# Eight rotating W2 buffers, and an output projection split into four full row tiles and a 64-row remainder

## The chip, the cores and the metric

The kernel runs on one core of one Trainium2 chip. The metric is the device time of one execution in microseconds (us): before the change 562.51 us, the median of three runs (562.33 to 562.85). A core has five engines that run their own instruction streams and meet through semaphores: TensorE (PE, with its weight loads listed apart as PEld), VectorE (DVE), ScalarE (ACT), GpSimd (POOL) and SyncE (SP), which here only issues DMAs. ACT issues DMAs as well.

## The reference

One transformer block in parallel form, with bf16 inputs: sequence S = 2048, width D = 576, H = 32 heads of Dh = 18, sliding window W = 256, feed-forward width F = 4608.

```python
xn = layernorm(x)
q, k, v = split(xn @ wqkv)                        # 32 heads of 18
p = softmax(mask(q @ k.T * 18**-0.5))             # causal, window of 256
attn = (p @ v) @ wo                               # output projection, 576 x 576
glu  = (silu(xn @ w1) * (xn @ w3)) @ w2           # 576 -> 4608 -> 576
out  = x + attn + glu
```

## The kernel before, in words

The sequence is cut into four chunks of 512 rows (c = 0 to 3). Each chunk goes through three stages on PE, and PE runs them strictly one after the other:

- **Projections** (`proj_part`, L437): q, k, v of the chunk from the normalised, transposed input `xnT`. The depth of 576 is handled as nine pieces of 64 rows; two matmuls of 64 rows each stand at array rows 0 and 64 (`tile_position`), write two different PSUM banks and run side by side. I call two such matmuls a pair.
- **Units** (`unit_pairs`, L664): 36 units per chunk, one for each 128 columns of W1 and W3; nine pairs of 512 columns each. Between the pairs the code lays single attention steps: `scores` (L557), `exps` on ACT (L566), `masks` on POOL (L593), and, when the exponentials of two head groups are there, a `pv` block (L614). `unit_tanh` (L673, ACT) and `unit_h` (L679, L682, DVE) turn the two PSUM banks of a unit into one 128-row slice of `hT`. Three PSUM jobs of two banks rotate over the units.
- **P2** (`p2_list` and `p2_item`, L687 to L731): the second feed-forward matmul and the output projection, summed in the same four PSUM banks `ACC[tt]` (tt = 0 to 3 are the blocks of 128 sequence rows). It makes two passes (`half` 0 and 1) over 288 output columns each. A pass runs through nine W2 tiles of 512 rows; a tile is 16 matmuls of 128 rows x 288 columns (L715). In the last tile of a pass each block tt is followed by five matmuls of the output projection (kd = 0 to 4, L721), and then by `out`: DVE adds the residual (L728) and SP stores it (L730).

**W2 tiles** (`load_w2`, L343): four buffers `w2[0..3]` of 288 KB. The first four loads of the program are issued on SP in units 20 to 26 of chunk 0; each later one on ACT, directly after the last matmul of the tile whose buffer it takes, so a load has three tiles of matmuls in which to land.

**W1/W3 tiles** (`load_part`, L312): 36 tiles, nine per chunk, each in six DMAs of 192 KB on SP, in rotating buffers `w13[0..2]`; the fourth tile of chunk 0 alone lands in a part of `hT` that is free then. The counter `owed` spreads the parts: each time a matmul group is put out (`owe_part`), one owed part is issued behind it. The last tile of every chunk lies in `w13[1]`; that buffer is filled again only in the projections of the next chunk, with the third tile of that chunk (first used in unit 8).

**The output projection's input** `oT` has five tiles of 128 partitions. `o_pack` (L639) moves four heads' 18-row blocks of the group pair j (0 to 3) at a time from `od` (two buffers) by DMA: seven blocks fill rows 0 to 125 of tiles 0 to 3, and the last four heads' rows lie in rows 0 to 71 of tile 4. The rest of `oT` and of the weights `wo` is zeroed by four memsets in units 8 to 11 of chunk 0 (L962), and `wo` is loaded in unit 13 by five DMAs.

The order on each engine is the order in which `add` is called in this Python program; there is no scheduler behind it. Waits are worked out from the readers and writers of each named buffer. DMAs that one engine issues are one queue; SP's queue therefore holds W1/W3 parts, the repacking of keys and queries (`span_issue`, L502), the packs of `oT`, x loads and stores in the order of the calls.

The change touches `load_w2`, `o_pack`, `p2_list`, `p2_item`, the calls in the main loop (L829 to L839, L849, L912 to L974) and the numbering of the P2 items (L982).

Of the kernel before, what the change touches and what calls it, by code (L numbers as in the profile page):

```python
# [5 lines left out]
dt = mybir.dt  # L6
# [158 lines left out]
def bass_parallel_sum__sliding_block__glu_gated_swiglu__prompt_kernel(  # L165
# [20 lines left out]
    G = H // 4  # L186
# [11 lines left out]
    with ExitStack() as es:  # L198
# [129 lines left out]
        def load_w13(behind=(), parts=6):  # L328
            for _ in range(parts):
                load_part((), behind)  # L330
# [7 lines left out]
                owed -= 1  # L338
                load_part((op,))

        n2fill = 0

        def load_w2(eng="sp"):  # L343
            nonlocal n2fill
            if n2fill >= NC * 2 * NFC:
                return
            s = n2fill % NW2
            half, fc = divmod(n2fill % (2 * NFC), NFC)
            n2fill += 1
            add(eng, lambda e: e.dma_start(  # L350
                w2[s][:], B_w2[fc * 512:(fc + 1) * 512, half * HD:(half + 1) * HD].rearrange("(fl p) d -> p fl d", p=128)),
                w=[("w2", s)], dma=f"w2_{s}")


        def ln_stats(t, s, part):
# [283 lines left out]
        def o_pack(j, eng):  # L639
            i = j % NOD  # L640
            first = True
            for q in range(4):
                m = 4 * j + q
                if m < 14:
                    t, r0 = 2 * (m // 7), Dh * (m % 7)
                    moves = [(oT[r0:r0 + Dh, t:t + 2, :], od[i][32 * q:32 * q + Dh, :, :])]
                else:
                    r0 = 2 * Dh * (m - 14)
                    moves = [(oT[r0 + Dh * p:r0 + Dh * (p + 1), 4, :], od[i][32 * q:32 * q + Dh, p, :]) for p in range(2)]
                for dst, src in moves:  # L650
                    add(eng, lambda e, dst=dst, src=src: e.dma_start(dst, src),
                        r=[("od", i), "oTz"], dma=f"oT{j}", **{"w" if first else "j": [("oT", j)]})
                    first = False

        def unit_pairs(c, u, n0, n1, b0):

# [30 lines left out]
        def p2_list(c):  # L687

            seq = []
            for half in range(2):  # L690
                base = c * 2 * NFC + half * NFC
# [12 lines left out]

        of_ctr = 0
# [1 line left out]
        def p2_item(c, item, xs):  # L707
            nonlocal of_ctr
            what, half, fc, k, tt, sl, last = item
            d0 = half * HD  # L710
            bank = PS[:, ACC[tt], 0:HD]
            key = [("ps", ACC[tt])]
            if what == "w2":
                f = fc * 4 + k
                add("pe", lambda e: e.matmul(  # L715
                    bank, hT[:, f, tt * 128:(tt + 1) * 128], w2[sl][:, k, :], start=(f == 0), stop=False),
                    r=[("h", f), ("w2", sl)], **{"w" if f == 0 else "j": key})
                if last:
                    load_w2("act")
            elif what == "wo":  # L720
                add("pe", lambda e: e.matmul(  # L721
                    bank, oT[:, k, tt * 128:(tt + 1) * 128], wo[:, k, d0:d0 + HD], start=False, stop=(k == 4)),
                    r=[("oT", j) for j in range(G // 2)] + ["oTz", "wo", "woz"], j=key)
            else:
                o = of_ctr % NOF
                of_ctr += 1
                t = c * TB + tt
                add("dve", lambda e: e.tensor_tensor(ofin[:, o, :], bank, xp[xs[tt]][:, d0:d0 + HD], ALU.add),  # L728
                    r=key + [("xp", xs[tt])], w=[("of", o)])
                add("sp", lambda e: e.dma_start(out2[t * 128:(t + 1) * 128, d0:d0 + HD], ofin[:, o, :]),  # L730
                    r=[("of", o)], dma=f"out{o}")  # L731
# [105 lines left out]
        main, rest = span_main, span_last  # L837
# [5 lines left out]
        for c in range(NC):  # L843
# [23 lines left out]
            def later(u, what):  # L867
                side.setdefault(u, []).append(what)
# [43 lines left out]
            for u in range(NF):  # L912
                at_u = u
                if c == 0 and u == 0:
                    owed += 12
                if u in loads:
                    for i in loads[u]:
                        xslot[(c + 1) * TB + i] = load_x((c + 1) * TB + i)
# [12 lines left out]
                if next_pv in pv_ready and clock >= pv_ready[next_pv] and next_pv < 3:  # L931
                    j = next_pv
                    next_pv += 1
                    banks = job()
                    pv(c, j, banks)
                    clock += PV_COST
                    for g in (2 * j, 2 * j + 1):
                        for s in range(NS):
                            if pt_of[(c, g, s)][0] != "h":
                                free.append(pt_of[(c, g, s)])  # L940
                    later(u, lambda b=banks: (pv_out(b[0], 0), pv_out(b[1], 1), o_scale(0)))
                    later(u + 1, lambda j=j: (o_turn(2 * j, 0), o_turn(2 * j, 1), o_scale(1)))
                    later(u + 2, lambda j=j: o_turn(2 * j + 1, 0))
                    later(u + 3, lambda j=j: (o_turn(2 * j + 1, 1), o_pack(j, "sp")))
                unit_h(u, b0[0])
                for what in side.pop(u, []):
                    what()
# [8 lines left out]
                    ln_apply(t, xslot[t])  # L956
                for span, a, b, n0, n1, eng in late_spans.get(u, []) if c == 0 else []:
                    span(a, b, only=slice(n0, n1), **({"q_eng": eng} if span is main else {"eng": eng}))
                if c == 0 and u in (8, 9, 10, 11):
                    buf, key = ((wo, "woz"), (oT, "oTz"))[(u - 8) // 2]  # L960
                    part = buf[64:128, 4, :] if u % 2 else buf[96:128, 0:4, :]
                    add("dve", lambda e, part=part: e.memset(part.bitcast(dt.float32), 0.0), **{"j" if u % 2 else "w": [key]})  # L962
                if c == 0 and u == 13:
                    for t in range(4):
                        rows = A_wo[252 * (t // 2):252 * (t // 2) + 252, :].rearrange("(s p d) f -> p s d f", p=2, d=Dh)[t % 2, :, :, :]
                        add("sp", lambda e, t=t, rows=rows: e.dma_start(wo[0:126, t, :], rows),
                            r=["woz"], dma="wo", **{"j" if t else "w": ["wo"]})
                    add("sp", lambda e: e.dma_start(wo[0:72, 4, :], A_wo[504:576, :]), r=["woz"], j=["wo"], dma="wo")
# [69 lines left out]
```

## Time and profile before

| what | value |
|---|---|
| time of three runs | 562.51 us median, 562.33 to 562.85 |
| time of the profiled execution | 562.53 us |
| its span in the profile | 560.8 us |
| time outside the span | 562.53 - 560.8 = 1.73 us |
| busy share PE / DVE / ACT / POOL | 99% / 56% / 45% / 29% |
| chunk 0: projections and start, units, P2 | 0 to 22.14, to 102.12, to 143.57 us |
| DMA traffic | 85.83 MB, mean 153 GB/s |

All times of the profile count from the start of the span. A row of a timeline reads: start, length, engine, line, operation, output<-inputs, partitions and columns, count. A row of the chain of waits reads: start, length, what. The length of a matmul group holds the tail of its last matmul (a 288-column matmul is listed with 286 ns, though the next one starts 122 ns later), so rates are read from starts.

### The profile page before, as it was taken

To read this page: it belongs to the slowest core of one execution; us is meant where nothing else is said; L and a number is where in the kernel's file an instruction comes from. 1 tells how busy PE (TensorE), PEld (TensorE's weight loads), DVE (VectorE), ACT (ScalarE), POOL (GpSimd) and SP (SyncE) were. 2 spreads that over 40 slices of the span, in tenths; PEclk is the share of its full clock that TensorE was granted. 3 is DMA by queue.
4 is the path that set the end of the run, shared out by engine and by line. 5 is a ranking of instruction groups with operands and counts; after the bars stand their busy time and mean duration, and the time that the engine had idled before them with its cause. 6 is when DMAs were issued, how large, how long until landed. Compare 5 with 4: busy or idle time off the path is not lost.

```text
span 560.8 us, 15711 instructions
## 1 busy us (share of the span) xinstructions
PE 555.4 (99%) x6767; PEld 343.9 (61%) x6767; DVE 314.8 (56%) x587; ACT 253.1 (45%) x349; POOL 163.1 (29%) x383
## 2 busy tenths in 40 slices
PE   8999999999999999999999999999999999999998
PEld 4445455677665455477766645547777654555776
DVE  7468788710465778851046668883114567767211
ACT  4357776100287776600037776650004676675000
POOL 6313454400034445330003344532000333433000
PEclk9999999999999999999999999999999999999999
DMA  9988879886366467587626754868752675460552
GB/s 249 206 192 179 198 171 203 196 215 176 87 143 145 117 146 165 139 200 206 170 67 139 169 129 111 161 177 189 194 145 59 138 172 131 113 162 12 139 148 64
DMA packets 126685, 85.83 MB, mean 153 GB/s; under 512 B 34024, under 2 KB 124320, under 8 KB 126616
## 3 DMA queue, kind: packets, MB, share of 16 engines
q1 hardware_dynamic: 89076, 63.16, 49.5%
q10 hardware_dynamic: 37540, 21.66, 14.7%
q8 instruction: 53, 0.87, 0.7%
q14 instruction: 16, 0.13, 0.1%
HBM read 71.29 MB, written 2.36 MB: 131 GB/s over the span
## 4 chain that ended last, share of the span: by engine, by line
PE 97%; DMA 2%; DVE 1%; issue 0%; POOL 0%
PE ps L664 50%; PE ps L715 24%; PE ps L437 9%; PE ps L557 6%; PE ps L614 4%; PE ps L721 3%; DMA w<-in_B_w_dram 1%; DMA xp<-in_A_x_dram 0%; DVE xn L370 0%; DVE stats L358 0%; DVE stats L360 0%; DVE mv L361 0%; POOL rstd L364 0%; PE ps L382 0%; DVE ofin L728 0%
## 5 line engine op out<-in xcount | busy, mean ns | idle before, releaser
L664 PE MATMUL ps<-xnT,w 64*128 64x512 bf16 x1400 | 181.3, 376 | 0.1
L664 PE MATMUL ps<-xnS,w 64*128 64x512 bf16 x1120 | 153.9, 376 | 0.0
L715 PE MATMUL ps<-w,hT 128*128 128x288 bf16 x1152 | 147.3, 286 | 0.2 <-DMA w<-in_B_w_dram 0.2
L566 ACT ACTIVATE pt<-ps 128x1024 bf16<-128x1024 f32 (+1 forms) x112 | 113.1, 1010 | 63.4 <-PE ps L557 63.1
L679 DVE SCALAR_TENSOR_TENSOR gs<-th,ps 128x512 bf16<-128x512 bf16 x144 | 97.8, 679 | 77.8 <-ACT th L673 76.7
L715 PEld LDWEIGHTS ps<-w,hT 128*128 128x128 bf16 x1152 | 111.9, 98 | 30.9 <-issue 1.7
L664 PEld LDWEIGHTS ps<-xnT,w 64*128 64x128 bf16 x1400 | 69.9, 94 | 58.6 <-issue 0.5
L593 POOL TENSOR_TENSOR pt<-pt,mk 128x128 int32<-128x128 int32 (+1 forms) x199 | 80.3, 425 | 79.5 <-ACT pt L566 79.5
L682 DVE SCALAR_TENSOR_TENSOR hT<-gs,ps 128x512 bf16<-128x512 bf16 x144 | 98.9, 687 | 5.0
L673 ACT ACTIVATE th<-ps 128x512 bf16<-128x512 f32 x144 | 85.4, 593 | 24.0 <-PE ps L664 23.7
L664 PEld LDWEIGHTS ps<-xnS,w 64*128 64x128 bf16 x1120 | 57.0, 94 | 52.5
L728 DVE TENSOR_TENSOR ofin<-ps,xp 128x288 bf16<-128x288 f32 x32 | 14.6, 457 | 120.2 <-PE ps L721 120.2
L450 ACT ACTIVATE stage<-ps 128x512 bf16<-128x512 f32 x16 | 9.6, 597 | 146.1 <-PE ps L437 143.8
L593 POOL TENSOR_TENSOR hT<-hT,mk 128x128 int32<-128x128 int32 (+1 forms) x31 | 12.4, 421 | 170.7 <-ACT hT L566 170.7
L557 PE MATMUL ps<-qv,kv 64*128 64x320 bf16 (+4 forms) x528 | 52.5, 260 | 0.0
L557 PEld LDWEIGHTS ps<-qv,kv 64*128 64x128 bf16 x528 | 27.3, 94 | 25.8 <-issue 0.3
L437 PE MATMUL ps<-xnT,wp 64*128 64x512 bf16 (+1 forms) x360 | 38.7, 355 | 0.0
L566 ACT ACTIVATE stage<-ps 128x1024 bf16<-128x1024 f32 x24 | 24.6, 1023 | 12.6 <-PE ps L557 12.6
L636 DVE STREAM_TRANSPOSE od<-oq 128x256 bf16<-128x256 bf16 x64 | 25.8, 427 | 6.3 <-POOL oq L629 6.3
L437 PEld LDWEIGHTS ps<-xnT,wp 64*128 64x128 bf16 x360 | 19.0, 94 | 14.1 <-issue 0.7
L721 PE MATMUL ps<-wo,oT 128*128 128x288 bf16 x160 | 24.8, 286 | 0.0
L593 POOL TENSOR_TENSOR stage<-stage,mk 128x128 int32<-128x128 int32 (+1 forms) x42 | 17.0, 423 | 17.4 <-ACT stage L566 17.2
(59 smaller groups left out, 341.9 us busy)
## 6 DMA issues: line engine op xcount, KB each, us to landing
w<-in_B_w_dram SPq DMA_DIRECT2D x210, 192.0 KB, 4.1
w<-in_B_w_dram ACTq DMA_DIRECT2D x68, 288.0 KB, 3.1
xp<-in_A_x_dram SPq DMA_DIRECT2D x29, 144.0 KB, 4.3
out_dram<-ofin SPq DMA_DIRECT2D x32, 72.0 KB, 1.7
xnS<-xnT SPq DMA_DIRECT2D x8, 256.0 KB, 4.3
oT<-od SPq DMA_DIRECT2D x56, 36.0 KB
pt<-in_A_wqkv_dram SPq DMA_DIRECT2D x4, 288.0 KB, 6.5
hT<-in_B_w_dram SPq DMA_DIRECT2D x6, 192.0 KB, 5.1
```

What stands on the lines that cost most here:

```text
L437: op = add("pe", lambda e, out_=out_, st=st, mv=mv, n=n, r0=r0, first=first: e.matmul(out_, st, mv, start=first, stop=(part == 1 and n == ...
L557: add("pe", lambda e, r0=r0, out_=out_, kb=kb, q0=q0, nb=nb: e.matmul(out_, kb4[r0:r0 + 64, g, kb + NV - NB, :] if kb < 0 else kv[r0:r0 + ...
L566: add("act", lambda e: e.activation(pt_slot(sl)[:, 0:w, :], PS[:, SC[0]:SC[1] + 1, 0:w].rearrange("p r q -> p q r"), ACT.Exp, scale=scale) ...
L593: add("pool", lambda e, vb=vb, mm=mm: e.tensor_tensor(vb, vb, mm, ALU.mult), r=(key if n == 0 else []) + ["mk"], **{"w" if n == 0 else "j" ...
L614: add("pe", lambda e, p=p, q=q, pr=pr, sl=sl, g=g, pos=pos, q0=q0, nb=nb, col=col, first=first, n=n: e.matmul(PS[32 * q:32 * q + VW, banks ...
L636: add("dve", lambda e: e.transpose(od[i][:, g % 2, c0:c0 + CH // 2], oq[:, c0:c0 + CH // 2]), r=["oq", "oq0"], **{"j" if half or g % 2 els ...
L664: op = add("pe", lambda e, n=n, r0=r0, r=r, k=k, src=src: e.matmul(PS[:, b0 + r, :], wt[r0:r0 + 64, k, fl * 128:(fl + 1) * 128], src, star ...
L673: add("act", lambda e: e.activation(th[i][:], PS[:, bg, :], ACT.Tanh, scale=0.5), r=[("ps", bg)], w=[("th", i)])
L679: add("dve", lambda e: e.scalar_tensor_tensor(out=gs[i][:], in0=th[i][:], scalar=1.0, in1=PS[:, bg, :], op0=ALU.add, op1=ALU.mult), r=[("t ...
L682: add("dve", lambda e: e.scalar_tensor_tensor(out=hT[:, u, :], in0=gs[i][:], scalar=0.5, in1=PS[:, bu, :], op0=ALU.mult, op1=ALU.mult), r= ...
L715: add("pe", lambda e: e.matmul(bank, hT[:, f, tt * 128:(tt + 1) * 128], w2[sl][:, k, :], start=(f == 0), stop=False), r=[("h", f), ("w2", ...
L721: add("pe", lambda e: e.matmul(bank, oT[:, k, tt * 128:(tt + 1) * 128], wo[:, k, d0:d0 + HD], start=False, stop=(k == 4)), r=[("oT", j) fo ...
```

## The change

- **W2 in eight buffers.** Four more tiles fit exactly into `w13[1]` (9 x 512 elements per partition = 4 x 4 x 288): `w2x`. Tile i of a chunk (i = 0 to 17 over both passes) has place i mod 8; places 0 to 3 are the old buffers (turned by two from chunk to chunk), places 4 to 7 lie in `w13[1]`. At the start of P2 the loads of tiles 4 to 7 are issued on ACT, all four at once, behind the last matmul of the units. After tile i's last matmul tile i + 8 is loaded; after tiles 10, 11, 16 and 17 tiles 0, 1, 2 and 3 of the next chunk.
- **Rows of the output projection dealt anew.** Tiles 0 to 3 of `oT` and `wo` now have 128 used rows (28 heads, and two rows each of the first four heads), tile 4 has the other 16 rows of these four heads: 64 rows. They are stored twice over in `wo` (rows 0 to 63 and 64 to 127); in `oT` an even block tt has them in rows 0 to 63 and an odd one in rows 64 to 127, with zeros in the other half.
- **The remainder as 64-row matmuls.** A new item `wr` is a matmul of 64 rows x 288 columns at array row 0 (tt even) or 64 (tt odd). In pass 0 the four `wr` open P2, right behind the units, and start the sums; in pass 1 of chunks 0 to 2 they close P2, right ahead of the next chunk's projections, and the four `out` come behind them. Pass 1 of chunk 3 keeps five full matmuls per block. The full matmuls (L721) fall from 160 to 132, and 28 `wr` come in.
- **Packs.** j = 0 takes 12 DMAs instead of 4 (8 of them move 16 rows of 2 x 128 columns); j = 3 takes 4 instead of 6. In chunk 0 the eight small ones are issued on ACT, one per unit, 4 to 11 units after the `pv` block; in the others on SP, two per unit.
- **Around it.** One memset of `oT` instead of four of `oT` and `wo`; seven DMAs for `wo` instead of five; W1/W3 tile 2 of chunk 0 is issued whole in the projections (where two x loads stood) and not over the first units; the two x loads move to units 11 and 13, the other two of that chunk to 15 and 17.

```diff
+        w2x = w13[1][:, :, :].rearrange("p a b -> p (a b)")[:, 0:NW2 * 4 * HD].rearrange("p (n k d) -> p n k d", n=NW2, d=HD)
+        def w2_at(c, i):
+            n = i % (2 * NW2)
+            if n < NW2:
+                s = (n + 2 * c) % NW2
+                return s, w2[s]
+            return n, w2x[:, n - NW2, :, :]
+        def load_w2(c, i, eng="act", after=()):
+            if c >= NC:
                 return
-            s = n2fill % NW2
+            s, dst = w2_at(c, i)
...
+        def next_w2(c, i):
+            if i < 10:
+                load_w2(c, i + 8)
+            elif i < 12:
+                load_w2(c + 1, i - 10)
+            elif i >= 16:
+                load_w2(c + 1, i - 14)
...
+        def by_par(ap, par):
+            return ap.rearrange("d (a b f) -> d a b f", b=2, f=128)[:, :, par, :]
+        def pack_moves(j):
             i = j % NOD
+            moves = []
             for q in range(4):
+                m = 4 * j + q - 2
+                if m >= 0:
                     t, r0 = 2 * (m // 7), Dh * (m % 7)
+                    moves.append((oT[r0:r0 + Dh, t:t + 2, :], od[i][32 * q:32 * q + Dh, :, :]))
                 else:
+                    moves.append((oT[126:128, 2 * q:2 * q + 2, :], od[i][32 * q:32 * q + 2, :, :]))
+            for n in range(4 if j == 0 else 0):
+                q, p = divmod(n, 2)
+                for par in range(2):
+                    r0 = 64 * par + 16 * n
+                    moves.append((by_par(oT[r0:r0 + 16, 4, :], par), by_par(od[i][32 * q + 2:32 * q + Dh, p, :], par)))
+            return moves
+        def o_pack(j, eng, n0=0, n1=4):
...
+                apart = half == 0 or c + 1 < NC
+                if half == 0:
+                    seq += [("wr", 0, 0, 0, tt, 0, False) for tt in range(TB)]
                 for fc in range(NFC):
-                    sl = (base + fc) % NW2
+                    sl = half * NFC + fc
...
-                            seq += [("wo", half, fc, kd, tt, sl, False) for kd in range(5)]
-                            seq.append(("out", half, fc, 0, tt, sl, False))
+                            seq += [("wo", half, fc, kd, tt, sl, False) for kd in range(4 if apart else 5)]
+                            if half == 0 or not apart:
+                                seq.append(("out", half, fc, 0, tt, sl, False))
+            if c + 1 < NC:
+                for what in ("wr", "out"):
+                    seq += [(what, 1, 0, 0, tt, 0, False) for tt in range(TB)]
...
+            elif what == "wr":
+                r0 = 64 * (tt % 2)
+                add("pe", lambda e: e.matmul(
+                    bank, oT[r0:r0 + 64, 4, tt * 128:(tt + 1) * 128], wo[r0:r0 + 64, 4, d0:d0 + HD],
+                    start=(half == 0), stop=(half == 1), tile_position=(r0, 0)),
+                    r=[("oT", 0), "oTz", "wo"], **{"w" if half == 0 else "j": key})
...
                 span_last(0, 2)
-                for t in (TB, TB + 1):
-                    xslot[t] = load_x(t)
+                load_w13()
...
+            if c == 0:
+                loads = {11: (0,), 13: (1,), 15: (2,), 17: (3,)}
...
-                    owed += 12
+                    owed += 6
...
+                    if j == 0:
+                        for n in range(4, 12, 1 if c == 0 else 2):
+                            later(u + n if c == 0 else u + n // 2 + 2,
+                                  lambda n=n: o_pack(0, "act", n, n + 1) if c == 0 else o_pack(0, "sp", n, n + 2))
...
-                if c == 0 and u in (8, 9, 10, 11):
-                    buf, key = ((wo, "woz"), (oT, "oTz"))[(u - 8) // 2]
-                    part = buf[64:128, 4, :] if u % 2 else buf[96:128, 0:4, :]
-                    add("dve", lambda e, part=part: e.memset(part.bitcast(dt.float32), 0.0), **{"j" if u % 2 else "w": [key]})
+                if c == 0 and u == 8:
+                    add("dve", lambda e: e.memset(oT[:, 4, :].bitcast(dt.float32), 0.0), w=["oTz"])
...
+                if c == 0 and u == 18:
+                    rows = A_wo[0:4 * Dh, :].rearrange("(n d) f -> n d f", d=Dh)
+                    add("sp", lambda e: e.dma_start(wo[126:128, 0:4, :], rows[:, 0:2, :].rearrange("n d f -> d n f")),
+                        j=["wo"], dma="wo")
+                    for p in range(2):
+                        add("sp", lambda e, p=p: e.dma_start(wo[64 * p:64 * p + 64, 4, :], rows[:, 2:Dh, :]),
+                            j=["wo"], dma="wo")
                 if c == 0 and u in (20, 22, 24, 26):
-                    load_w2()
+                    load_w2(0, (u - 20) // 2, "sp")
...
+            for i in range(NW2, 2 * NW2):
+                load_w2(c, i, after=(last_pe(),))
             banks = ()
-            for n, item in enumerate(p2_list(c)):
+            for n, item in enumerate(p2_list(c), -TB):
```

More of the change, by code (lines that the diff above doesn't have):

```diff
@@ L339, in owe_part @@
                 load_part((op,))
[L341 to L345, printed above, removed]
+        w2x = w13[1][:, :, :].rearrange("p a b -> p (a b)")[:, 0:NW2 * 4 * HD].rearrange("p (n k d) -> p n k d", n=NW2, d=HD)
[7 more added lines that the diff above has]
+            if c >= NC:
                 return
-            s = n2fill % NW2
-            half, fc = divmod(n2fill % (2 * NFC), NFC)
-            n2fill += 1
+            s, dst = w2_at(c, i)
+            half, fc = divmod(i, NFC)
             add(eng, lambda e: e.dma_start(
-                w2[s][:], B_w2[fc * 512:(fc + 1) * 512, half * HD:(half + 1) * HD].rearrange("(fl p) d -> p fl d", p=128)),
-                w=[("w2", s)], dma=f"w2_{s}")
+                dst[:, :, :], B_w2[fc * 512:(fc + 1) * 512, half * HD:(half + 1) * HD].rearrange("(fl p) d -> p fl d", p=128)),
+                w=[("w2", s)], after=after, dma=f"w2_{s}")
+        def next_w2(c, i):
[5 more added lines that the diff above has]
+                load_w2(c + 1, i - 14)
         def ln_stats(t, s, part):
@@ L637, in o_turn @@
                 r=["oq", "oq0"], **{"j" if half or g % 2 else "w": [("od", i)]})
-        def o_pack(j, eng):
+        def by_par(ap, par):
+            return ap.rearrange("d (a b f) -> d a b f", b=2, f=128)[:, :, par, :]
+        def pack_moves(j):
             i = j % NOD
-            first = True
+            moves = []
             for q in range(4):
-                m = 4 * j + q
-                if m < 14:
+                m = 4 * j + q - 2
+                if m >= 0:
                     t, r0 = 2 * (m // 7), Dh * (m % 7)
-                    moves = [(oT[r0:r0 + Dh, t:t + 2, :], od[i][32 * q:32 * q + Dh, :, :])]
+                    moves.append((oT[r0:r0 + Dh, t:t + 2, :], od[i][32 * q:32 * q + Dh, :, :]))
                 else:
[L648 to L653, printed above, removed]
+                    moves.append((oT[126:128, 2 * q:2 * q + 2, :], od[i][32 * q:32 * q + 2, :, :]))
[6 more added lines that the diff above has]
+        def o_pack(j, eng, n0=0, n1=4):
+            for n, (dst, src) in list(enumerate(pack_moves(j)))[n0:n1]:
+                add(eng, lambda e, dst=dst, src=src: e.dma_start(dst, src),
+                    r=[("od", j % NOD), "oTz"], dma=f"oT{j}", **{"j" if n else "w": [("oT", j)]})
         def unit_pairs(c, u, n0, n1, b0):
@@ L690, in p2_list @@
             for half in range(2):
-                base = c * 2 * NFC + half * NFC
+                apart = half == 0 or c + 1 < NC
+                if half == 0:
+                    seq += [("wr", 0, 0, 0, tt, 0, False) for tt in range(TB)]
                 for fc in range(NFC):
-                    sl = (base + fc) % NW2
+                    sl = half * NFC + fc
                     edge = fc == NFC - 1 or (half == 1 and fc == 0)
@@ L714, in p2_item @@
                 f = fc * 4 + k
+                buf, wt = w2_at(c, sl)
                 add("pe", lambda e: e.matmul(
-                    bank, hT[:, f, tt * 128:(tt + 1) * 128], w2[sl][:, k, :], start=(f == 0), stop=False),
-                    r=[("h", f), ("w2", sl)], **{"w" if f == 0 else "j": key})
+                    bank, hT[:, f, tt * 128:(tt + 1) * 128], wt[:, k, :], start=(f == 0 and half == 1), stop=False),
+                    r=[("h", f), ("w2", buf)], **{"w" if f == 0 and half == 1 else "j": key})
                 if last:
-                    load_w2("act")
+                    next_w2(c, sl)
             elif what == "wo":
                 add("pe", lambda e: e.matmul(
-                    bank, oT[:, k, tt * 128:(tt + 1) * 128], wo[:, k, d0:d0 + HD], start=False, stop=(k == 4)),
-                    r=[("oT", j) for j in range(G // 2)] + ["oTz", "wo", "woz"], j=key)
+                    bank, oT[:, k, tt * 128:(tt + 1) * 128], wo[:, k, d0:d0 + HD], start=False,
+                    stop=(k == (3 if half == 0 else 4))),
+                    r=[("oT", j) for j in range(G // 2)] + ["oTz", "wo"], j=key)
+            elif what == "wr":
[4 more added lines that the diff above has]
+                    r=[("oT", 0), "oTz", "wo"], **{"w" if half == 0 else "j": key})
             else:
```

6 lines of the change are left out of this document (3 added, 3 removed).

## The prediction

> **What bounds the kernel now.** I read the page first: busy shares, the chain of waits, then the groups that the change touches.
>
> ```profile
> span 560.8 us, 15711 instructions
> ...
> PE 555.4 (99%) x6767; PEld 343.9 (61%) x6767; DVE 314.8 (56%) x587; ACT 253.1 (45%) x349; POOL 163.1 (29%) x383
> ...
> PEclk9999999999999999999999999999999999999999
> ...
> PE 97%; DMA 2%; DVE 1%; issue 0%; POOL 0%
> ...
> L721 PE MATMUL ps<-wo,oT 128*128 128x288 bf16 x160 | 24.8, 286 | 0.0
> ```
>
> PE is busy for 99% of the span, the chain of waits is 97% PE, and the granted clock is full in every slice. So the time moves only if PE gets less to do, or if a place where PE stands still goes or comes. The mean of 286 ns for an output-projection matmul is its length to the end of its tail, not its price. The price is read from starts, in the chain of waits around the second pass of chunk 2:
>
> ```profile
> 399.57 1.97 PE ps L715 x16
> ...
> 401.56 6.05 DMA w<-in_B_w_dram
> ...
> 407.65 8.50 PE ps L715 x68
> 416.16 0.61 PE ps L721 x5
> ```
>
> Five matmuls in 0.61 us and sixteen in 1.97 us: 0.122 us each, the price of a full matmul of 288 columns. The same rows show a real stop: a W2 tile issued at 401.56 landed 6.05 us later, and PE went on at 407.65. How long PE stood is in the timeline of PE there:
>
> ```profile
> 402.83 4.57 PE L715 MATMUL ps<-w,hT 128*128 128x288 bf16 x36
> 407.65 4.58 PE L715 MATMUL ps<-w,hT 128*128 128x288 bf16 x36 [0.25 <-DMA w<-in_B_w_dram]
> ```
>
> The first group ends at 407.40, so its last matmul started 0.286 earlier, at 407.11; the next was due at 407.24 and came at 407.65: 0.41 us lost. The idle time shown, 0.25, is smaller because the tail counts as busy.
>
> **The change part by part**, against the profiled execution: 562.53 us, of which 560.8 is the span and 1.73 lies outside; it stands 0.02 over the median of 562.51, so the sum serves for both.
>
> *1. The remainder as pairs.* Full matmuls fall from 160 to 132: 28 x 0.122 = 3.42 us removed. The 28 new matmuls of 64 rows make 14 pairs (two passes of chunks 0 to 2, one of chunk 3, two pairs each). The nearest rows for a pair of 288 columns are the v projections, in the timeline behind chunk 0's P2:
>
> ```profile
> 142.87 0.78 PE L721 MATMUL ps<-wo,oT 128*128 128x288 bf16 x5
> 143.57 3.20 PE L437 MATMUL ps<-xnT,wp 64*128 64x512 bf16 x28
> 146.60 0.78 PE L437 MATMUL ps<-wv,xnT 64*128 64x288 bf16 x10
> ...
> 149.16 1.29 PE L437 MATMUL ps<-wv,xnT 64*128 64x288 bf16 x18
> 150.26 2.13 PE L437 MATMUL ps<-xnT,wp 64*128 64x512 bf16 x18
> ```
>
> Eighteen start between 149.16 and 150.26: nine pairs in 1.10 us, 0.122 per pair; each loads its own weights, as `wr` does. Added: 14 x 0.122 = 1.71 us. **Net 1.71 us gained.** The bounds: 3.42 if a pair cost nothing, 0 if the two ran one behind the other. I take 1.71, since rows, columns, banks and array rows are those of the row shown.
>
> *2. Switching between 128-row and 64-row work.* The five L721 matmuls start at 142.87, the last at 142.87 + 4 x 0.122 = 143.36; the projections start 0.21 later instead of 0.12: a switch costs 0.09 us. The way into P2 is the other direction:
>
> ```profile
> 101.81 0.38 PE L664 MATMUL ps<-xnT,w 64*128 64x512 bf16 x2
> 102.12 1.15 PE L715 MATMUL ps<-w,hT 128*128 128x288 bf16 x8
> ```
>
> The unit's last pair starts at 101.81, and a pair of 512 columns takes 0.216 (0.122 x 512/288), so again 0.09 too much. The change adds no switch: pass 0's `wr` stand between the units (64 rows) and the W2 tiles, pass 1's between L721 and the projections (64 rows); each boundary only moves by two pairs. Taken: 0; above, 14 x 0.09 = 1.3 us if every group paid two more. The Trainium skill, page "TensorEngine Tiling (Array Packing)", section "Tiling Modes", says that a change of tiling mode, unlike a change of tile, drains TensorE; the trace agrees with its 0.09, and by that rule too this placement pays nothing more, while in the middle of a pass the 1.3 would eat three quarters of part 1.
>
> *3. What `wr` waits for.* In pass 0 they need the four banks, which the first W2 tile needed at the same moment before, and rows packed long ago. In pass 1 the four `out` now come in a row behind P2:
>
> ```profile
> L728 DVE TENSOR_TENSOR ofin<-ps,xp 128x288 bf16<-128x288 f32 x32 | 14.6, 457 | 120.2 <-PE ps L721 120.2
> ```
>
> 4 x 0.457 = 1.83 us on DVE. The first to want one of these banks is the first v projection, 3.0 us behind P2's end (143.57 to 146.60 above), and DVE's first projection copy has its data no sooner. Hidden with 1.2 us to spare; cost 0.
>
> *4. Waits for W2.* Besides the 0.41 us there is one more, in chunk 0:
>
> ```profile
> 112.78 4.40 PE L715 MATMUL ps<-w,hT 128*128 128x288 bf16 x34
> ...
> 115.04 1.95 PEld L715 LDWEIGHTS ps<-w,hT 128*128 128x128 bf16 x17 [0.20 <-DMA w<-in_B_w_dram]
> ```
>
> 34 matmuls start between 112.78 and 117.18 - 0.286 = 116.89: 33 steps of 0.122 make 4.03, and 4.11 passed, so some 0.07 lost. With eight buffers a load has seven tiles (7 x 16 x 0.122 = 13.7 us) instead of three (5.9 us) to land, against the 6.05 seen. Both waits go: **0.48 us gained**. Bounds: 0 if they come back elsewhere, 0.48 if not; I take 0.48. What is late next is the burst of tiles 4 to 7 (part 5).
>
> *5. Tiles 4 to 7, issued together at P2's start.* They wait on ACT for the last unit's matmul, as the last tanh before them does; behind them ACT has nothing until the next projections. In the queues beside them:
>
> ```profile
> 100.74 3.69 SPq L323 DMA_DIRECT2D w<-in_B_w_dram  x4
> 105.82 1.26 SPq L323 DMA_DIRECT2D w<-in_B_w_dram  x2
> ...
> 102.12:112.12 10.00, 10.00 (x147) 7.87 (x146) 6.22 (x14) 0.60 (x1) 4.74 (x11) 1.00 0.95 202
> ```
>
> (The last row is that of the stages; its last column is GB/s.) Four tiles of 288 KB and six parts of 192 KB are 2.3 MB, 11.5 us at 202 GB/s, all of it together. Tile 4 is needed after 64 matmuls (7.8 us) and the PV block, tile 7 after 112 (13.7 us). Tiles land in order of issue, so I expect no wait: 0. Above, see the slow rival. The Trainium skill, "DMA: Bandwidth & Descriptors", section "Issuing engines are not separate DMA queues", speaks against the burst: DMAs of all issuers run on the same 16 engines and interleave. By it tile 4 could have to share with SP's parts; at half of 202 GB/s it lands after an estimated 3 us and tile 7 after 11.5, and the sum stays as it is. The sharing is seen here in the 6.05 us.
>
> *6. W1/W3 tile 2 of chunk 0 earlier.* The chain of waits over the first units:
>
> ```profile
> 22.14 12.95 PE ps L664 x120
> ...
> 35.31 1.73 PE ps L664 x16
> ...
> 37.26 0.86 PE ps L664 x8
> 38.12 0.07 issue
> 38.20 1.04 PE ps L664 x8
> ```
>
> 120 + 16 + 8 = 144 matmuls are eight units, so the stop lies ahead of unit 8, the first on tile 2. PE's timeline and SP's queue:
>
> ```profile
> 35.58 1.24 PE L664 MATMUL ps<-xnT,w 64*128 64x512 bf16 x10
> ...
> 37.75 1.49 PE L664 MATMUL ps<-xnT,w 64*128 64x512 bf16 x10
> ```
> ```profile
> 32.50 2.87 SPq L323 DMA_DIRECT2D w<-in_B_w_dram  x2
> ```
> ```profile
> w<-in_B_w_dram SPq DMA_DIRECT2D x210, 192.0 KB, 4.1
> ```
>
> Ten such matmuls take 1.24, here 1.49: 0.25 lost. Tile 2's last part is the second of the two issues from 32.50 on; with 4.1 us to landing it comes at about 38. In the changed order its six parts stand right behind the keys of groups 0 and 1, four issues earlier, and wait for no matmul: **0.24 us gained** (0 to 0.25). What is pushed back on SP by some 1.5 us are keys of groups 2 to 4, needed from the ninth score step on, over ten units later; x loads, two tiles before their statistics.
>
> *7. Small packs on ACT in chunk 0.* Eight issues on an engine that also runs a tanh and about one exponential per unit. The nearest rows:
>
> ```profile
> 35.36 1.02 ACT L566 ACTIVATE hT<-ps 128x1024 bf16<-128x1024 f32 x1 [0.92 <-PE ps L557]
> 36.01 0.77 ACTq L502 DMA_DIRECT2D qv<-stage  x1
> 36.28 0.59 ACT L673 ACTIVATE th<-ps 128x512 bf16<-128x512 f32 x1
> 37.30 1.02 ACT L566 ACTIVATE hT<-ps 128x1024 bf16<-128x1024 f32 x1 [0.43 <-PE ps L557]
> ```
>
> The issue ran from 36.01 to 36.78 while the tanh ran from 36.28 to 36.87, and the next exponential waited for PE. So an issue behind a tanh lies beside it: cost 0. The first of the eight also waits for DVE's last turn of that pair; behind it stand an exponential and the next tanh, and PE waits for them only if the exponential comes later than the next score step, one unit on. Above: if nothing overlapped, 0.77 - 0.43 = 0.34 over the free time of a unit, eight times, 2.7 us.
>
> *8. The rest.* DVE loses three memsets; SP gets eight more pack issues in chunks 1 to 3, ahead of W1/W3 parts that are needed two tiles later, and two for `wo`. All of it lies beside PE's units: 0.
>
> **Sum:** 562.53 - 1.71 - 0.48 - 0.24 = **560.1 us**, 0.4% less.
>
> **The rivals.**
>
> *The waits stay.* The 0.48 and 0.24 come back at another load. For: DMA is 95% busy after 102.12. Against: every load named is issued earlier. Then 1.71 alone: 560.8.
>
> *The pairs don't run side by side.* Then 28 x 0.122 come back in for the 28 removed, and 0.72 is left: 561.8. Against: the v projections.
>
> *ACT becomes the bound in eight units of chunk 0:* 560.1 + 2.7 = 562.8. For: only 0.43 us free per unit; against: the overlap shown.
>
> *Slower: the burst lands too slowly.* Place: the fourth to seventh W2 tile of a pass 0. Tile 7 is needed 13.7 us after P2's start, so it decides at 13.7 / 4 = 3.4 us per tile in the ACT queue. At 4.5 us each tile 7 lands at 18.0 and PE stands 4.3 us; in chunk 0 alone that gives 564.4, in all four 577.3. For: single tiles have taken 6.05 beside other traffic. Against: that is a latency; the rate of 202 GB/s brings everything in 11.5 us.
>
> **How the numbers follow.** Chances: forecast 0.66, waits stay 0.12, pairs one by one 0.08, ACT 0.06, burst 0.08. The range holds the first three: from 559.6 (the forecast and a scatter of half a microsecond, the spread of the three runs) to 561.9. About 0.2% (1.1 us) is what a measurement of this kernel can tell from no change: 561.4 and below is faster, so 0.66 + 0.12 = 0.78; the pairs and ACT cases are the same, 0.14; slower 0.08.
>
> **What would show it.** Right: `wr` start two by two, 0.12 us per pair; first W2 matmul behind them with the same 0.09; no idle time of the P2 loads put down to a DMA; ten matmuls at unit 8 in 1.24 us; the span at 558.4. Wrong: PE idle ahead of tiles 4 to 7; gaps between score steps in units 18 to 26 of chunk 0; a stop at the v projections behind P2.

## The result, and the profile after

The changed kernel takes **560.88 us** (median of 8 runs, 560.29 to 561.63) against 562.49 before (8 runs, 562.33 to 563.09): ratio 0.9971, 95% interval [0.9962, 0.998]. It is faster by 1.6 us, inside the stated range and 0.8 us short of the 560.1 forecast. Its runs spread over 1.3 us, those of before over 0.8.

The page of the changed kernel (span, busy shares, chain of waits by engine and line, DMA issues with KB and median time to landing); lines have moved: L686 are the units, L744 the W2 tiles, L750 the full output projection, L756 the new `wr`, L674 the packs.

```profile
span 559.1 us, 15730 instructions
...
PE 554.5 (99%) x6767; PEld 346.9 (62%) x6767; DVE 311.8 (56%) x584; ACT 253.0 (45%) x349; POOL 163.4 (29%) x383
...
PE 95%; DMA 2%; DVE 1%; SPq 0%; POOL 0%; issue 0%
PE ps L686 50%; PE ps L744 23%; PE ps L450 9%; PE ps L570 6%; PE ps L627 4%; PE ps L750 3%; DMA oT<-od 1%; DMA xp<-in_A_x_dram 0%; SPq L674 0%; PE ps L756 0%; DVE xn L383 0%; POOL oq L642 0%; DVE od L649 0%; DVE stats L371 0%; DVE stats L373 0%
...
w<-in_B_w_dram SPq DMA_DIRECT2D x210, 192.0 KB, 4.3
w<-in_B_w_dram ACTq DMA_DIRECT2D x68, 288.0 KB, 5.7
```

PE's share of the chain fell from 97% to 95%, and "DMA oT<-od" is new in it: the packs. The last row says why to look at DMAs: a W2 tile now takes 5.7 us from issue to landing, where the same row of before had 3.1:

```profile
w<-in_B_w_dram ACTq DMA_DIRECT2D x68, 288.0 KB, 3.1
```

The new wait in the timeline of the changed kernel, at the end of chunk 0's pass 0:

```profile
117.79 1.76 PE L744 MATMUL ps<-w,hT 128*128 128x288 bf16 x13
119.97 0.37 PEld L750 LDWEIGHTS ps<-wo,oT 128*128 128x128 bf16 x4 [0.73 <-issue]
120.00 0.65 PE L750 MATMUL ps<-wo,oT 128*128 128x288 bf16 x4 [0.45 <-DMA oT<-od]
```

and in its chain of waits:

```profile
112.15 0.70 SPq L674
112.85 0.04 issue
112.89 6.97 DMA oT<-od
119.86 0.14 issue
120.00 0.65 PE ps L750 x4
```

The W2 group's last matmul started at 119.55 - 0.286 = 119.26; the first output projection was due 0.12 later and came at 120.00, so 0.61 us are lost. The last pack of the last group, issued at 112.89, landed 6.97 us later. Before, the trace has these packs landing 2.5 to 3.65 us after their issue, the last of them at 116.88, 2.6 us ahead of its use at 119.47.

There is a second new stop, in chunk 2:

```profile
387.97 2.07 PEld L744 LDWEIGHTS ps<-w,hT 128*128 128x128 bf16 x18 [0.38 <-issue]
```

By the starts of the matmuls it costs 0.24 us. It stands in the middle of a W2 tile (at the 74th matmul of the pass), and no semaphore is named.

### The profile page after: what moved, and what is told of

Read it like the earlier page. It is cut to its first block, busy times and chain, and to the rows that moved or that the text cites. A ratio compares the mean times of both kernels' runs of the same rounds, so it can differ in the third digit from the quotient of the medians.

```text
span 559.1 us, 15730 instructions
## 1 busy us (share of the span) xinstructions
PE 554.5 (99%) x6767; PEld 346.9 (62%) x6767; DVE 311.8 (56%) x584; ACT 253.0 (45%) x349; POOL 163.4 (29%) x383
## 4 chain that ended last, share of the span: by engine, by line
PE 95%; DMA 2%; DVE 1%; SPq 0%; POOL 0%; issue 0%
PE ps L686 50%; PE ps L744 23%; PE ps L450 9%; PE ps L570 6%; PE ps L627 4%; PE ps L750 3%; DMA oT<-od 1%; DMA xp<-in_A_x_dram 0%; SPq L674 0%; PE ps L756 0%; DVE xn L383 0%; POOL oq L642 0%; DVE od L649 0%; DVE stats L371 0%; DVE stats L373 0%
## 5 line engine op out<-in xcount | busy, mean ns | idle before, releaser
L686 PE MATMUL ps<-xnT,w 64*128 64x512 bf16 x1400 | 181.9, 376 | 0.0
L686 PE MATMUL ps<-xnS,w 64*128 64x512 bf16 x1120 | 154.9, 376 | 0.0
L744 PE MATMUL ps<-w,hT 128*128 128x288 bf16 x1152 | 147.3, 286 | 0.1
L744 PEld LDWEIGHTS ps<-w,hT 128*128 128x128 bf16 x1152 | 112.0, 98 | 29.9 <-issue 1.5
L686 PEld LDWEIGHTS ps<-xnT,w 64*128 64x128 bf16 x1400 | 72.5, 94 | 56.3
L686 PEld LDWEIGHTS ps<-xnS,w 64*128 64x128 bf16 x1120 | 59.0, 94 | 51.1
L642 POOL TENSOR_TENSOR oq<-uq,rden 128x288 bf16<-128x288 f32 x16 | 10.8, 674 | 39.0 <-DVE rden L641 39.0
```

The costliest lines, as they stand in the source:

```text
L686: op = add("pe", lambda e, n=n, r0=r0, r=r, k=k, src=src: e.matmul(PS[:, b0 + r, :], wt[r0:r0 + 64, k, fl * 128:(fl + 1) * 128], src, star ...
L744: add("pe", lambda e: e.matmul(bank, hT[:, f, tt * 128:(tt + 1) * 128], wt[:, k, :], start=(f == 0 and half == 1), stop=False), r=[("h", f ...
```

## The experiments

The theory at the outset: the pairs and the earlier W1/W3 tile bring what was forecast; loading W2 eight tiles ahead fills the queues of the shared DMA engines, and the small packs wait in them. The main rival: the new dealing of rows and its order on SP make the packs late. Each kernel was timed beside the kernel before, whose median was 562.66 in the first four, 562.45 in the next four and 562.89 in the last three. The stops are read from the starts of the matmuls in one profiled execution of each; the last column has those in P2 and at unit 8, from 0.1 us on. A tile's lead is the time of the matmuls between the issue of its load and its first use.

| kernel | median us | ratio to before, 95% | stops of PE behind the start, us |
|---|---|---|---|
| changed | 560.88 | 0.9971 [0.9962, 0.998] | packs 0.61; "issue" 0.24 |
| four buffers | 560.52 | 0.9962 [0.995, 0.9974] | W2 tile 0.28 |
| eight alone | 566.12 | 1.0064 [1.0048, 1.008] | packs 0.76, 1.27, 1.14 |
| six ahead, no wait | 561.77 | 0.9984 [0.9975, 0.9993] | packs 0.72, 0.42; "issue" 0.23 |
| five ahead, no wait | 561.14 | 0.9974 [0.9964, 0.9984] | packs 0.70 |
| five ahead, waiting | 560.20 | 0.9958 [0.9945, 0.997] | none |
| four, then seven | 560.78 | 0.9968 [0.9955, 0.998] | W2 tile 0.31, 0.25 |
| one by one | 562.11 | 0.9994 [0.9985, 1.0003] | none |
| middle of the pass | 561.38 | 0.9979 [0.997, 0.9989] | W2 tile 0.21, 0.25 |
| tile 2 late | 560.69 | 0.9964 [0.9952, 0.9976] | unit 8: 1.40 |
| five ahead alone | 562.68 | 1.0008 [0.9991, 1.0024] | unit 8: 0.68; "issue" 0.58 |
| PV earlier | 560.45 | 0.9956 [0.9944, 0.9968] | "issue" 0.40 |

**Four buffers** (the changed kernel without the eight buffers).

```diff
-            n = i % (2 * NW2)
...
+            s = (2 * NFC * c + i) % NW2
+            return s, w2[s]
...
+            c2, i2 = divmod(2 * NFC * c + i + NW2, 2 * NFC)
+            load_w2(c2, i2)
...
-            for i in range(NW2, 2 * NW2):
-                load_w2(c, i, after=(last_pe(),))
```

> The changed kernel with W2 in the four old buffers (each load behind the tile whose buffer it takes), all else as changed. Theory (the eight buffers load too far ahead; the backlog on the DMA engines makes the packs of oT's last group land late, 6.97 us instead of about 3, and PE stops 0.61 us at the first output projection of chunk 0, and 0.24 us in chunk 2): the packs land in 2 to 4 us, no stop at the output projection, the W2 waits of before (0.06 and 0.41 us) are back; 562.5 - 1.7 - 0.24 = 560.5 to 560.7. Rival (the new dealing of the rows and its SP order make the packs late, not the W2 loads): the stop of 0.6 us stays in this kernel as well, 561.1 to 561.3.

Measured 560.52. The packs of chunk 0 land 2.5 to 3.2 us after their issue and the stop at the output projection is gone; in its chain of waits one old W2 wait is left:

```profile
400.11 5.91 DMA w<-in_B_w_dram
406.02 0.05 issue
406.07 5.93 PE ps L744 x47
```

As the theory said, and against the rival: the dealing is the same here. In the median, this kernel is not slower than the changed one (the intervals of the two ratios overlap): a gain from the eight buffers, as loaded there, is not to be seen.

**Eight alone** (the kernel before, with the eight buffers and nothing else).

```diff
-                    load_w2("act")
+                    next_w2(c, sl)
...
+            for i in range(NW2, 2 * NW2):
+                load_w2(c, i, after=(last_pe(),))
```

> The kernel before with W2 in eight buffers, loaded as in the changed kernel, and nothing else. Theory: the W2 waits (0.48 us) go and a stop of about 0.6 us or more at the first output projection of chunk 0 comes, so nothing is gained: 562.4 to 562.9, same. Rival (the dealing makes the packs late): no stop, 562.0. The prediction's part 4 alone: 562.0.

Measured 566.12 (six runs, 564.78 to 568.33): slower than before, and far more than expected. The direction is the theory's, the size is not: the first output projection waits in chunks 0, 1 and 2. PE's timeline in chunk 1:

```profile
256.80 2.12 PE L727 MATMUL ps<-w,hT 128*128 128x288 bf16 x16
260.04 0.77 PE L733 MATMUL ps<-wo,oT 128*128 128x288 bf16 x5 [1.11 <-DMA oT<-od]
```

Here the last group has six packs instead of four; the last of them is issued 2.1 us later (115.03 against 112.89 in chunk 0) and still takes 5.64 us to land. So the change's own dealing, with four packs, had softened what its buffers did.

**Six ahead and five ahead, without a wait.** Only the distance in `next_w2` and the number of tiles loaded at the start of P2 were changed (shown for five; the other kernel has 6 in both places):

```diff
-            if i < 10:
-                load_w2(c, i + 8)
+            if i + 5 < 2 * NFC:
+                load_w2(c, i + 5)
...
-            for i in range(NW2, 2 * NW2):
+            for i in range(NW2, 5):
```

> The changed kernel with the same eight buffers, but loads six tiles ahead: only tiles 4 and 5 at the start of P2, then tile i+6 behind tile i; the next chunk's first two tiles behind tiles 14 and 15. Theory: less in the queues when the packs are issued, they land in 4 to 5.5 us, the stop at the output projection is gone or under 0.1 us, no W2 wait: 560.1 to 560.3. Rival (dealing): the stop stays, 560.9.

> As the six-ahead kernel, but five tiles ahead: tile 4 alone at the start of P2, then tile i+5 behind tile i (lead of four tiles, 7.8 us, against the 6.05 us that a tile took at worst before). Theory: the packs land in 3 to 4.5 us, no stop, no W2 wait: 560.1 to 560.2, the best of the four. Rival (dealing): 560.9. If the lead is too short, a W2 wait of some tenths shows: 560.4.

Measured 561.77 and 561.14, both with the stop. That looked like the rival, but the trace of the five-ahead kernel shows four W2 issues on ACT from 102.28 to 104.39, as in the changed kernel (101.97 to 104.33): places 5 to 7 had not been read in this chunk, so no wait held their loads, and ACT ran through them at once. ACT's timeline has nine issues in the first 12 us of its P2, where the next kernel, with a wait, has six (five ahead first, then the waiting version):

```profile
102.28 12.03 ACTq L355 DMA_DIRECT2D w<-in_B_w_dram  x9
```
```profile
101.91 11.61 ACTq L355 DMA_DIRECT2D w<-in_B_w_dram  x6
```

The kernels didn't do what they say; they are two more cases of the burst. It is worth the reader's care: in a program whose waits come from readers and writers, the place of a DMA in the order paces it only if something makes it wait.

**Five ahead, waiting.** The same, with the last matmul as an explicit reason to wait:

```diff
+            for j in [i + 5] if i < 13 else [] if i < 14 else [i + 4]:
+                load_w2(c + j // 18, j % 18, after=(last_pe(),))
...
+            for i in range(NW2, 5):
```

> The changed kernel with loads five tiles ahead, now held by a wait: tile 4 at the start of P2, then tile i+5 issued only after the last matmul of tile i (in the two kernels before this one no wait held tiles 5 to 7, whose places nobody had read in this chunk, and all four went out at once as in the changed kernel). Theory (backlog on the shared DMA engines): each load is only one tile earlier than with four buffers, the packs land in 3 to 4.5 us, no stop at the output projection, no W2 wait: 560.0 to 560.3. Rival (the engines are full through pass 0, so whatever is loaded earlier is queued ahead of the packs): packs 4.5 to 6 us, a stop of 0.1 to 0.4 us: 560.4 to 560.8.

Measured 560.20, five runs within 0.17 us, and not one stop in P2. Its page and its chain of waits at the place of the stop (L743 are the W2 tiles, L749 the output projection):

```profile
span 558.2 us, 15730 instructions
...
PE 98%; DVE 1%; DMA 0%; POOL 0%; issue 0%
```
```profile
107.96 11.52 PE ps L743 x94
119.47 0.49 PE ps L749 x4
119.96 0.49 PE ps L743 x4
```

The packs of chunk 0 land in 3.9 to 4.9 us. A W2 tile lands in 3.4 (median):

```profile
w<-in_B_w_dram ACTq DMA_DIRECT2D x68, 288.0 KB, 3.4
```

What differs from the changed kernel is not the traffic. The stage rows of both (changed first; the last three columns are clock, DMA share and GB/s) move 233 GB/s over the 20 us from P2's start:

```profile
102.12:122.12 20.00, 19.55 (x224) 15.24 (x223) 6.91 (x15) 0.44 (x1) 4.57 (x11) 1.00 1.14 233
```
```profile
102.12:122.12 20.00, 20.00 (x227) 15.80 (x228) 7.00 (x16) 0.38 (x1) 4.49 (x11) 1.00 1.13 233
```

What differs is how many W2 tiles are in flight when the last pack of this group is issued, and with it how long the packs take: five tiles and 6.6 to 7.0 us in the changed kernel, three and 3.9 to 4.9 here, two and 2.5 to 3.2 with four buffers.

Part of this may be a wait in SP's own queue. Two W1/W3 parts of 192 KB stand there ahead of the packs, and the last of them landed 10.5 us after its issue in the changed kernel (at 116.88; the first pack followed at 117.25), 6.6 us here and 5.2 with four buffers. No run put the packs ahead of these parts or in another queue, so how much of the delay is a pack's own and how much its place behind them stays open; both grew with the W2 tiles in flight.

The five runs lie below all eight of the changed kernel (560.25 at most against 560.29 at least), but the intervals of the two ratios still overlap, and "four buffers" and "PV earlier" have ratios as low. In the trace of the waiting version the pairs run and none of these stops is left; that it is the fastest version is not shown.

**Four ahead, then seven.**

```diff
+            for j in [i + 4] if i < 9 else {9: [13, 14], 10: [15, 16], 11: [17], 14: [18], 15: [19], 16: [20], 17: [21]}.get(i, []):
+                load_w2(c + j // 18, j % 18, after=(last_pe(),))
```

> Eight places, but loads four tiles ahead through pass 0 as with four buffers, and from tile 9 on up to seven ahead, when the packs are used up. Theory: no stop at the output projection (as with four buffers), and the W2 wait of 0.28 us in pass 1 of chunk 2 that the four buffers left is gone: 560.0 to 560.3, the fastest of all. Rival (it is not the lead but the eight buffers as such, or chance): no better than four buffers, 560.5.

Measured 560.78: a miss. No stop at the packs, but tile 13 comes late twice. It is still loaded four tiles ahead, now with tile 14 right behind it, beside the stores and the 512 KB for `xnS`, and took 5.95 and 5.88 us to land. A lead has to be longer when the traffic comes, not afterwards.

**One by one** (the four-buffer version with all 64-row matmuls at array row 0; the remainder of the odd blocks is left out of its result).

```diff
-                r0 = 64 * (tt % 2)
+                r0 = 0
```

> The four-buffer version of the changed kernel (560.5) with every 64-row matmul of the remainder at array row 0, so that no two can run side by side; odd blocks then read zeros, so their 64 rows are left out of the result. Theory (the gain is the pairing): 14 x 0.122 = 1.7 us more, 562.2. Rival (a 64-row matmul is cheaper by itself): 560.5 to 561.4.

Measured 562.11, 1.6 above the four buffers, and the intervals of the ratios lie apart. The four starts of a group now lie 122 to 134 ns apart each instead of 3, 119 to 130 and 3. The gain of part 1 is the pairing: a 64-row matmul alone is no cheaper than a full one.

**Middle of the pass** (the four-buffer version, `wr` of pass 0 behind the third W2 tile).

```diff
-                if half == 0:
-                    seq += [("wr", 0, 0, 0, tt, 0, False) for tt in range(TB)]
...
+                    if half == 0 and fc == 2:
+                        seq += [("wr", 0, 0, 0, tt, 0, False) for tt in range(TB)]
```

> The four-buffer version of the changed kernel (560.5) with the remainder of pass 0 put behind the third W2 tile and not ahead of the first. Theory (each change between 64-row and 128-row work costs 0.09 us): two more changes in each of four chunks, 8 x 0.09 = 0.75 us more, 561.2, and 216 ns instead of 122 on each side in the trace. Rival (place does not matter): 560.5.

Measured 561.38, 0.86 above the four buffers, with intervals that just overlap, so the trace has to decide; it has 0.18 us of larger W2 waits besides the switches. PE's timeline shows the price on both sides:

```profile
107.79 1.39 PE L744 MATMUL ps<-w,hT 128*128 128x288 bf16 x10
109.11 0.42 PE L756 MATMUL ps<-wo,oT 64*128 64x288 bf16 x4
109.46 2.75 PE L744 MATMUL ps<-w,hT 128*128 128x288 bf16 x21
```

The last W2 matmul starts at 107.79 + 9 x 0.122 = 108.89, `wr` 0.22 later; between the starts the trace has 218 ns into the 64-row work and 215 out of it, in all four chunks, instead of 122.

**Tile 2 late** (the five-ahead, waiting version with W1/W3 tile 2 as before).

```diff
-                load_w13()
+                for t in (TB, TB + 1):
+                    xslot[t] = load_x(t)
...
-                    owed += 6
+                    owed += 12
```

> The five-ahead version with a wait (560.2) with W1/W3 tile 2 of chunk 0 loaded over the first units again, and the two x loads back in the projections. Prediction's part 6: the stop of 0.24 us ahead of unit 8 is back: 560.4 to 560.5. Rival (the stop at unit 8 had another cause, or the two x loads cost something where they now stand): 560.2.

Measured 560.69 in another group of runs than the 560.20; the intervals of the ratios overlap, so the times alone do not tell the two apart. The trace does: the stop ahead of unit 8 is back, and in this execution larger than before the change. PE goes on 0.09 us after the last part of tile 2 landed (39.41), as it did before the change (38.11 and 38.20). Its PE timeline:

```profile
37.88 0.38 PE L685 MATMUL ps<-xnT,w 64*128 64x512 bf16 x2
39.50 1.04 PE L685 MATMUL ps<-xnT,w 64*128 64x512 bf16 x8 [1.24 <-issue]
```

**Five ahead alone** (the kernel before with the eight buffers, loaded as in the waiting version).

```diff
-                    load_w2("act")
+                    next_w2(c, sl)
...
+            for i in range(NW2, 5):
+                load_w2(c, i, after=(last_pe(),))
```

> The kernel before with W2 in eight buffers, loaded five tiles ahead with the wait, and nothing else. Theory (only the size of the lead makes the packs late): no stop at the output projection, although this kernel has six packs of the last group and not four, and none of the W2 waits of 0.06 and 0.41 us: 562.0. Rival (with six packs any lead is too much): a stop of some tenths, 562.3 or more, against 566.1 with the loads eight ahead.

Measured 562.68, the same as before, where the theory had 562.0; the twelve runs spread from 562.04 to 567.88, so 0.5 us could not have been seen. No stop at the packs, even with six of them, and no W2 wait, as the theory said. In the profiled execution 0.68 us went at unit 8 (this kernel loads tile 2 late) and 0.58 at an "issue" stop in chunk 2, near the place of the one above.

**PV earlier** (the changed kernel, loads as they are, the last PV block, whose result the packs move, ten matmuls earlier).

```diff
-                elif n == 19:
+                elif n == 9:
```

> The changed kernel, loads eight ahead as they are, with the last PV block of each chunk ten matmuls (1.2 us) earlier in P2, so that the four packs are issued 1.2 us earlier. Theory (PE stops because the packs land late): the stop at the output projection goes, while the W2 loads stay as they are: 560.2 to 560.4. Rival (the stop comes with the backlog wherever the packs stand): it stays at 0.3 to 0.6 us, 560.9.

Measured 560.45, the stop gone: the packs of chunk 0 still take 6.4 to 6.8 us, but the last one is issued 0.7 us earlier (112.17) and lands 0.95 us ahead of its use; in chunk 1 the last lands only 0.14 us ahead. A W2 tile takes 6.2 us there:

```profile
w<-in_B_w_dram ACTq DMA_DIRECT2D x68, 288.0 KB, 6.2
```

So lateness of the packs is what stops PE at the output projection, and there are two cures: issue them earlier, or keep fewer W2 tiles in flight.

## Why the prediction was right, point by point

The gain came from where the prediction put it, and the time lies in its range. That it lies 0.8 us above the forecast has a cause that no part of the sum held (points 4 and 5); the range covered it only because it was drawn to hold losses of other kinds, which is partly luck. None of the signs that were to show a miss names the packs.

1. **Pairs: right, by its mechanism.** In PE's timeline of the changed kernel:

```profile
142.53 0.65 PE L750 MATMUL ps<-wo,oT 128*128 128x288 bf16 x4
143.12 0.42 PE L756 MATMUL ps<-wo,oT 64*128 64x288 bf16 x4
143.38 3.19 PE L450 MATMUL ps<-xnT,wp 64*128 64x512 bf16 x28
```

The two pairs that close P2 take 143.38 - 143.12 = 0.26 us, 0.13 per pair; by the starts of the matmuls 0.128, and 0.122 for the eight pairs that open P2. Net 28 x 0.122 - 8 x 0.122 - 6 x 0.128 = 1.67 us, forecast 1.71. "One by one" lost the same 1.6.

2. **Switches: right.** None was added (0.22 from L750's last start, 142.90, to `wr`), and "middle of the pass" confirms that two more cost 0.19 per chunk.

3. **`out` in a row behind P2: right.** No gap ahead of the first v projection (146.40, 3.0 us behind 143.38, as before). A later one waits 0.14 us at 149.58, but for ACT's copy, not for `out`, and the projections of this chunk take 13.63 us against 13.61 before.

4. **Waits for W2: half right.** The two waits of 0.06 and 0.41 are gone in the changed kernel. That they "come back elsewhere" was the lower bound and the rival with 0.12, and a loss did come: not at another load, as the rival had it, but 0.61 at the packs, and 0.24 at the "issue" stop, whose cause is open. That the rival's 560.8 is what was measured is partly luck: it takes back 0.72 (parts 4 and 6), while those stayed gained and 0.85 were lost elsewhere.

5. **The burst: the step that failed.** It asked whether tiles 4 to 7 themselves land in time, and they did: tile 7 landed 11.4 us after the first W2 matmul, as the sum of bytes had it (11.5). "What is late next is the burst of tiles 4 to 7" was wrong: late were other transfers beside and behind them, the four packs of the last group on SP. The prediction had looked at the new packs of group 0 and not at the old ones of group 3. Their slack was 2.6 us before, and about 4 with four packs instead of six, since the last is issued 1.5 us earlier; the burst took 4.5 (6.97 us to landing instead of 2.5).

6. **W1/W3 tile 2: right.** In the changed kernel the ten matmuls at unit 8 take their normal 1.24 us:

```profile
37.75 1.24 PE L686 MATMUL ps<-xnT,w 64*128 64x512 bf16 x10
```

Tile 2's last part landed at 34.95 here, 38.11 before. The 0.24 us were one execution's: in the four profiles with tile 2 loaded late the stop was 0.24, 0.68, 1.40 and, in "eight alone", nothing, since PE came to unit 8 later than the tile.

7. **Small packs on ACT: right.** They take 0.59 to 0.73 us and lie beside a tanh or an exponential. In ACT's timeline:

```profile
65.43 0.66 ACTq L674 DMA_DIRECT2D oT<-od  x1
65.43 0.59 ACT L695 ACTIVATE th<-ps 128x512 bf16<-128x512 f32 x1
66.29 1.02 ACT L579 ACTIVATE pt<-ps 128x1024 bf16<-128x1024 f32 x1 [0.26 <-PE ps L570]
```

The next exponential waits for PE, not for the issue. Behind the first of the eight it did start only when the issue had ended (64.57, 64.62), the case that the prediction had named; PE has no gap in these units.

The sum from these parts: 1.67 + 0.48 + 0.24 - 0.61 - 0.24 = 1.54 us, against 1.7 of the span. The rest, some 0.15 us, is spread over the units and has no single place. The waiting version, without the two losses, stands at 560.20, near the forecast's own sum of 560.1.

## What to carry to other kernels

Loading further ahead moved the wait here from the tiles' own matmuls to the packs, which share the DMA engines with them: before deepening a prefetch, list the small transfers that are issued while it runs, with their slack, not only the transfers that are deepened. A lead just over the worst landing seen left no stop, where the longest that fits did; but the landing itself grows with the lead. Before the change tiles took up to 6.2 us to land; loaded five ahead the tightest took 7.1 of a lead of 7.6, so 0.5 us were left; loaded eight ahead one took 12.1 of 13.9. And an issue is paced by a wait, not by its place in the program: look in the trace whether it was held.

## What the runs showed of the hardware

At the same 233 GB/s over 20 us, five W2 tiles in flight instead of three took packs of 36 KB from 3.9 to 4.9 us up to 6.6 to 7.0, and a W1/W3 part ahead of them from 6.6 to 10.5, although SP issues these and ACT the tiles. The Trainium skill, "DMA: Bandwidth & Descriptors", section "Issuing engines are not separate DMA queues", says that all issuers' DMAs run on the same 16 engines and interleave; the runs agree, and it was the sentence to follow to the packs.

Open: the stop put down to "issue" in chunk 2, at the 74th matmul of a pass (the 77th in "five ahead alone"). It came in four profiles (0.23 to 0.58 us). The trace holds transfers of instructions, 16 KB each, 53 in every profile. In all four the 37th of them begins 2.5 to 2.8 us before PE goes on. In the nine profiles without the stop it begins 2.7 to 6.3 us before PE passes the same place, so PE never passes it sooner than 2.5 us after the transfer's start. This fits late instructions that stop PE there, but no run moved the transfer, so the cause is not shown.
